# Softmax of a sparse attention: exponential by blocks on ScalarE, with bias and sum

## Chip, cores and metric

One core of one Trainium2 chip. The metric is the device time of one execution in microseconds, the median of the runs. The engines are named as in the profile: PE (matrix product), DVE (vector), ACT (scalar, activations), POOL (GpSimd) and SP (which only issues transfers here).

## What is computed

Attention with two sparse masks over 4 batches, 8 heads, 576 positions and 64 channels, and behind it four experts, each two matrix products, on the 2,304 rows that come out.

```python
def _attn_ref(q, k, v):
    B, H, S, D = q.shape
    stride, scale = 32, 1.0 / np.sqrt(D)
    scores = scale * np.matmul(q, k.transpose(0, 1, 3, 2))
    rel = pos[:, None] - pos[None, :]
    mask_local = (rel >= 0) & (rel < stride)
    mask_strided = (rel >= 0) & (pos[None, :] % stride == pos[:, None] % stride)
    scores = np.where(masks, scores, -1000000000.0)      # heads 0-3 local, 4-7 strided
    scores = scores - np.max(scores, axis=-1, keepdims=True)
    attn = np.exp(scores)
    attn = attn / (np.sum(attn, axis=-1, keepdims=True) + 1e-09)
    return np.matmul(attn, v)

def _moe_ref(x, domain_probs, w1, w2):
    p = domain_probs / (domain_probs.sum(-1, keepdims=True) + 1e-09)
    for e in range(E):
        h = np.maximum(x @ w1[e], 0.0)
        out += p[:, e:e + 1] * (h @ w2[e])
```

## The kernel before

The attention is cut into 16 pairs (n in the code), each two heads of one batch: "L" pairs with the local mask, "S" pairs with the strided one. `plan_pair` plans the work of one pair. Because the masks are sparse, a pair computes only small blocks of scores: an L pair has 9 blocks of 128 rows by 63 keys, an S pair 12 blocks of 128 rows by 54 keys. The softmax of a pair is worked in two groups, of 6 and 3 blocks (L) or 6 and 6 (S), so there are 32 groups in all. The tile pm (pmL or pmS, two buffers of each kind) holds the blocks of a pair, mx their row maxima, sm their row sums.

The steps of a group are, by the names of the functions: `scores` (small matmuls on PE into one or two banks of the pool sc), `mask` (DVE adds the mask, out of PSUM into pm, L541), `rmax` (DVE, the row maxima, L544), `bsub` (DVE or POOL subtracts the maximum of its row, L547), `ex` (ACT, one exponential over the whole group with the factor scale, L551), `rsum` (DVE, the row sums and their reciprocals, L556 to L559; the 1e-9 is an extra column of pm that is set at the start), `norm` (DVE or POOL multiplies by the reciprocal, L562). Then PE transposes three blocks at a time (`tp`, L592), ACT or DVE copies them to pT (`ep`, L452 or L454), PE multiplies with v (`pv`, L622 and L630), and the outcome is copied out as input of the experts.

Of the 2,304 rows the first 384 are worked first, by three-pass products on a high and a low half of each number: xh (the copy on ACT, L671) and xl (the remainder on DVE, L674). The channels of a row come from four pairs, xh_215 to xh_218. The weights are loaded to raw_202 (first layer) and raw_203 (second layer) and split likewise: s_80 and a_77 to a_79 for the first layer, w2t for the second (ACT, then DVE or POOL, L706 and L707). L801 is the first-layer product of these 384 rows, hs its ReLU (L805, L808), and L817 the second-layer product. In the first pass over the weights the channels are taken one after the other in the order of the pairs, so that the products can begin before all four pairs are done. The other rows (896 and 1,024) are worked by a scheme with seven half-size products (L970), once the attention is complete.

A planner in the kernel (`Plan`) sets the order in which the instructions are issued on every engine. Each step is added with its engine, its assumed duration, what it reads and writes and a priority; `walk` replays the engines with these durations and each engine takes what can start first, by priority. Attention steps and MoE steps take turns on PE by a running credit (MIX, SWING). A step of kind VP goes to DVE or POOL, one of kind AD to ACT or DVE, whichever is done sooner by the assumed times. A table SHIFT moves single steps by their number. As long as PE has nothing to do in the start, the planner puts in dummy matmuls on a tile wz, "fillers" (L1282). The order that comes out is fixed when the program is built; every engine then works its own list in that order.

Of the kernel before, what the change touches and what calls it, by code (L numbers as in the profile page):

```python
# [11 lines left out]
AF = mybir.ActivationFunctionType  # L12
# [4 lines left out]

MIX = 0.85
ZN = 30
# [5 lines left out]

LEAD = 8.24
LAG = 1.8
STEADY = 30.04


SHIFT = {
# [6 lines left out]
}  # L38
# [6 lines left out]
class Plan:  # L45
# [8 lines left out]
    DEEP = 1.27  # L54
    ROW = 1.98
    SWITCH = 0.17
    FIRST = 10
    SWING = 4.72
    ENGINES = ("PE", "ACT", "DVE", "POOL", "SP")
# [269 lines left out]
def attn_moe_kernel(  # L329
# [130 lines left out]
    def plan_pair(n):  # L460
# [19 lines left out]

        def pmv(g0, g1, eps=0):
            if kd == "S":
                return pmx[:, g0:g1, 0:W]
            a = pmx[:, P * g0 + 1 - eps:P * g0 + 2 - eps]
            return bass.AP(a.tensor, a.offset, [list(a.ap[0]), [3 * P, (g1 - g0) // 3], [P + 32, 3], [1, W + eps]])

# [11 lines left out]
        for gi, (g0, g1) in enumerate(GRP[kd]):  # L498
# [34 lines left out]
            def mask(key, g0, g1):  # L533
                ng = g1 - g0
                s = held[key][:, 0:ng * W]
                if kd == "S":
                    m, s = m_str.unsqueeze(1).to_broadcast([P, ng, SR]), s.rearrange("p (g w) -> p g w", w=W)
                else:
                    m = m_loc[:, 0 if g0 == 0 else 3:3 if g0 == 0 else 6, :].rearrange("p (v r) w -> p v r w", r=3)
                    s = s.rearrange("p (v r w) -> p v r w", r=3, w=W)  # L540
                nc.vector.tensor_tensor(out=pmv(g0, g1), in0=s, in1=m, op=ALU.add)  # L541

            def rmax(g0=g0, g1=g1):
                nc.vector.tensor_reduce(out=rows(mx, g0, g1), in_=pmv(g0, g1), op=ALU.max, axis=AX.X)  # L544

            def bsub(e, g0=g0, g1=g1, ng=ng):
                engine(e).tensor_tensor(  # L547
                    out=pmv(g0, g1), in0=pmv(g0, g1), in1=per(mx, g0, g1), op=ALU.subtract)

            def ex(g0=g0, g1=g1):  # L550
                nc.scalar.activation(out=pmv(g0, g1), in_=pmv(g0, g1), func=AF.Exp, scale=scale)  # L551

            def rsum(g0=g0, g1=g1):
                r = sm[:, par, g0:g1]
                if kd == "L":
                    nc.vector.tensor_reduce(out=rows(sm, g0, g1), in_=pmv(g0, g1, 1), op=ALU.add, axis=AX.X)  # L556
                else:
                    nc.vector.tensor_reduce(out=r, in_=pmx[:, g0:g1, 0:W + 1], op=ALU.add, axis=AX.X)
                nc.vector.reciprocal(out=r, in_=r)  # L559
# [8 lines left out]
            if kd == "S" and gi == 0:  # L568
                add("PE", 0.9, scores, [f"qkS{bf}{i}" for i in range(2)], keys + [f"pmS{bf}{i}" for i in range(2)], z + 3, keys,
                    cols=4 * nel)  # L570
            elif kd == "L":
                add("PE", (0.5, 0.46)[gi], scores, [f"qkL{bf}{gi}"], keys + [tok], z + 3, keys, cols=4 * nel)
            for i, x in enumerate(keys if kd == "L" else [key]):
                a0, a1 = (g0 + 3 * i, g0 + 3 * i + 3) if kd == "L" else (g0, g1)
                add("DVE", (a1 - a0) * W / 960 + 0.15, lambda x=x, a0=a0, a1=a1: mask(x, a0, a1), [x, "mask" + kd], [tok], z + 3.2)
            add("DVE", dd, rmax, [tok], [tm], z + 3.4)
            add("VP", vp, bsub, [tm], [tok], z + 3.6)
            add("ACT", nel / 1200 + 0.2, ex, (), [tok], z + 3.8)
            add("DVE", dd + 0.25, rsum, [tok], [ts], z + 4)
            add("VP", vp, norm, [ts], [tok], z + 4.2)  # L580

# [21 lines left out]
        for gi in range(2):  # L603
# [56 lines left out]
            if kd == "L":  # L660
                add("PE", 0.15 + 0.165 * ng, pv, need + [f"vstL{bf}{gi}"], keys, z + 7, keys, cols=ng * 288)
            elif gi == 0:
                add("PE", 0.95, pv, need + [f"vstS{bf}{i}" for i in range(2)], keys, z + 7, keys, cols=ng * 182)
            for (t0, nt, nm) in ((0, TA, "x"), (T0[1], TBS[0], "r1"), (T0[2], TBS[1], "r2")):
# [619 lines left out]
    with tc.manual_schedule():  # L1284
        nc.vector.memset(wz, 0.0)
        make_identity(nc, ident)
        for t in pm["S"]:
            nc.gpsimd.memset(t[:, :, SR + 1:64], 0.0)
            nc.gpsimd.memset(t[:, :, SR:SR + 1], 1e-9)
        for t in pm["L"]:  # L1290
            nc.gpsimd.memset(t, 0.0)
            a = t[:, 0:1]
            nc.gpsimd.memset(bass.AP(a.tensor, a.offset, [list(a.ap[0]), [3 * P, 3], [P + 32, 3], [1, 1]]), 1e-9)
        plan.run(idle)
# [76 lines left out]
```

## Time and profile before

| | us |
|---|---|
| median of 3 runs | 795.29 (795.02 to 797.27) |
| profiled execution, its own time | 795.16 |
| its span, first to last instruction | 793.4 |
| PE busy | 784.8 |
| DVE busy | 602.7 |
| POOL busy | 366.1 |
| ACT busy | 330.6 |

The own time of the profiled execution is 1.8 us longer than its span, which runs from the first to the last instruction. Busy times are shares of the span that an engine spends in instructions; idle time of an engine that is not waited for costs nothing. Rows of a trace give starts in microseconds from the start of the span; where neighbours on one engine overlap, the distance from start to start is shorter than a row's duration.

### The profile page before, as it was taken

The page shows a single profiled execution, that of the slowest core. Times are in us where ns is not written, and L with a number is a line of the kernel's source. Part 1 is how long each engine was busy: PE and PEld are TensorE (multiplying, and loading weights), DVE is VectorE, ACT ScalarE, POOL GpSimd, SP SyncE. Part 2 cuts the span into 40 slices and gives each one's busy share as a digit, 9 for nine tenths or more (in the row PEclk, how much of TensorE's full clock was granted, in tenths as well). Part 3 has the DMA queues.
Part 4 walks back from the last instruction along what each step waited for, and adds up shares of the span by engine and source line. Part 5 has one row for each costly group of instructions (what it writes and reads, how often), then busy time and mean ns, then how long its engine had stood idle before and what let it go on. Part 6 is the DMA issues. An engine that isn't in the chain of part 4 may idle for free.

```text
span 793.4 us, 13252 instructions
## 1 busy us (share of the span) xinstructions
PE 784.8 (99%) x5038; PEld 667.8 (84%) x5038; DVE 602.7 (76%) x854; ACT 330.6 (42%) x617; POOL 366.1 (46%) x289
## 2 busy tenths in 40 slices
PE   8999999999999999999999999999999999999998
PEld 5887889889888888898988888888888887888886
DVE  6987877774888686867778593958787868687986
ACT  4656556442635344363535352524141423232330
POOL 6555227650665152534435270708180817171672
PEclk9999999999999999999999999999999999999999
DMA  9586443366769786875863405837384746455525
GB/s 344 197 315 217 163 154 107 109 220 233 271 243 332 248 322 217 311 252 227 296 219 99 182 32 183 293 135 272 134 272 148 243 161 238 176 196 190 181 79 186
DMA packets 70431, 166.59 MB, mean 210 GB/s; under 512 B 5184, under 2 KB 23776, under 8 KB 70368
## 3 DMA queue, kind: packets, MB, share of 16 engines
q1 hardware_dynamic: 70224, 165.63, 59.1%
q8 instruction: 40, 0.66, 0.3%
q14 instruction: 23, 0.19, 0.1%
q10 hardware_dynamic: 144, 0.11, 0.1%
HBM read 105.94 MB, written 59.79 MB: 209 GB/s over the span
## 4 chain that ended last, share of the span: by engine, by line
PE 97%; DMA 1%; DVE 1%; issue 0%; ACT 0%
PE mo L970 22%; PE mo L817 18%; PE ps L970 17%; PE sc L970 15%; PE mo L801 9%; PE ps L817 5%; PE sc L817 5%; PE ps L592 2%; PE ps L630 1%; DMA ring<-d23s 1%; PE sc L529 1%; PE ps L622 1%; PE sc L517 1%; PE mo L1282 1%; DVE wv L707 0%
## 5 line engine op out<-in xcount | busy, mean ns | idle before, releaser
L1035 POOL TENSOR_TENSOR q<-q,q 128x512 f32<-128x512 f32 x41 | 60.9, 1492 | 143.1 <-DVE q L1004 142.2
L817 PE MATMUL mo<-w2t,h 128*128 128x512 f32 x336 | 80.8, 389 | 0.0
L817 PEld LDWEIGHTS mo<-w2t,h 128*128 128x128 f32 x336 | 63.1, 188 | 13.0
L817 PE MATMUL mo<-w2t,hs 128*128 128x512 f32 x288 | 70.0, 396 | 0.0
L808 DVE SCALAR_TENSOR_TENSOR h<-c,h 128x448 fp32r<-128x448 f32 x48 | 60.6, 1289 | 2.3 <-ACT h L805 1.0
L817 PEld LDWEIGHTS mo<-w2t,hs 128*128 128x128 f32 x288 | 52.9, 188 | 11.2 <-DVE hs L808 0.3
L706 ACT ACTIVATE w2t<-raw 128x512 fp32r<-128x512 f32 x60 | 37.2, 630 | 44.1 <-PE mo L817 29.0
L1084 DVE TENSOR_TENSOR acc<-sc,acc 128x512 f32<-128x512 f32 x58 | 39.1, 685 | 17.1 <-PE sc L970 17.0
L1001 DVE TENSOR_TENSOR q<-ps,v 128x512 f32<-128x512 f32 x48 | 33.1, 690 | 25.0 <-PE ps L970 24.8
L707 POOL TENSOR_TENSOR a<-raw,a 128x512 fp32r<-128x512 f32 x17 | 27.0, 1590 | 53.3 <-DVE c L1173 38.4
L826 DVE SCALAR_TENSOR_TENSOR acc<-mo,pr,acc 128x512 f32<-128x512 f32 x45 | 33.6, 747 | 23.2 <-PE mo L817 23.1
L707 POOL TENSOR_TENSOR w2t<-raw,w2t 128x512 fp32r<-128x512 f32 x20 | 28.6, 1436 | 44.9 <-ACT w2t L706 43.9
L992 ACT ACTIVATE v<-mo 128x512 f32<-128x512 f32 x48 | 28.5, 593 | 48.3 <-PE mo L970 48.3
L801 PE MATMUL mo<-xh,a 128*128 128x384 f32 x192 | 45.7, 341 | 0.0
L1004 DVE SCALAR_TENSOR_TENSOR q<-q,pb 128x512 f32<-128x512 f32 x48 | 42.8, 891 | 1.6
L706 ACT ACTIVATE wv<-tmp 128x512 fp32r<-128x512 f32 x32 | 20.1, 631 | 53.7 <-POOL tmp L714 11.0
L817 PE MATMUL ps<-w2t,h 128*128 128x512 f32 x168 | 40.4, 389 | 0.0
L817 PE MATMUL sc<-w2t,h 128*128 128x512 f32 x168 | 40.4, 389 | 0.0
L1030 ACT ACTIVATE Tb11h<-q 128x512 fp32r<-128x512 f32 x16 | 10.0, 628 | 71.2 <-DVE q L1004 71.2
L707 DVE TENSOR_TENSOR w2t<-raw,w2t 128x512 fp32r<-128x512 f32 x40 | 34.1, 881 | 4.9 <-ACT w2t L706 4.8
L1035 DVE TENSOR_TENSOR q<-q,q 128x512 f32<-128x512 f32 x23 | 32.7, 1420 | 6.7 <-POOL Tb21l L1031 6.5
L817 PEld LDWEIGHTS ps<-w2t,h 128*128 128x128 f32 x168 | 31.5, 188 | 6.5
(272 smaller groups left out, 2089.9 us busy)
## 6 DMA issues: line engine op xcount, KB each, us to landing
raw<-in_w SPq DMA_DIRECT2D x28, 1024.0 KB, 5.8
qkS<-in_qk_strided SPq DMA_DIRECT2D x16, 329.0 KB, 5.4
out<-acc SPq DMA_DIRECT2D x18, 256.0 KB, 2.0
qkL<-in_qk_local SPq DMA_DIRECT2D x8, 400.0 KB, 6.6
vstL<-in_v_local SPq DMA_DIRECT2D x8, 384.0 KB, 6.1
vstS<-in_v_strided SPq DMA_DIRECT2D x8, 384.0 KB, 7.4
pb<-dp SPq DMA_DIRECT2D x5, 512.0 KB, 7.4
raw<-in_w SPq DMA_DIRECT2D x4, 512.0 KB, 7.8
```

Of the source, the lines that this page charges most:

```text
L706: add("ACT", 0.62, lambda: nc.scalar.activation(out=hi(), in_=src(), func=AF.Copy), need, [name + "h"], z)
L707: add("VP", VP, lambda e: engine(e).tensor_tensor(out=lo(), in0=src(), in1=hi().bitcast(F32), op=ALU.subtract), need + [name + "h"], [name ...
L801: nc.tensor.matmul(pt[:, 0:TA], w[:, c % 2, (f % 2) * P:(f % 2) * P + P], (xl if i == 1 else xh)[c], start=j == 0, stop=j == 11)
L808: nc.vector.scalar_tensor_tensor(out=dst(), in0=src(), scalar=0.0, in1=hi().bitcast(F32), op0=ALU.max, op1=ALU.subtract)
L817: nc.tensor.matmul(pt, ht[f][:, ts], wt[f][:, cs], start=j == 0, stop=j == 11)
L826: nc.vector.scalar_tensor_tensor(out=a, in0=pt, scalar=sc, in1=a, op0=ALU.mult, op1=ALU.add)
L970: nc.tensor.matmul(pt, a[i == 2][:, j, f * P:f * P + P], skewed(b[i == 1][j], TH), start=bool(first) and n == 0, stop=True, skip_group_che ...
L992: add("ACT", TH2 / 1200 + 0.18, lambda: nc.scalar.activation(out=late["u"][i], in_=held[key][:, 0:TH2], func=AF.Copy), [key, "late3"], [f" ...
L1001: add("DVE", DD, lambda: nc.vector.tensor_tensor(out=q(), in0=src(), in1=late["u"][i], op=ALU.add), [key, f"u{i}", "late3"], [tok], min(zz ...
L1004: add("DVE", DD, lambda: nc.vector.scalar_tensor_tensor(out=q(), in0=q() if from_q else src(), scalar=0.0, in1=late["p"][:, c * TH2:c * TH ...
L1035: add("VP", VP, lambda e: engine(e).tensor_tensor(out=dst[0](), in0=a[0](), in1=b[0](), op=ALU.subtract), [a[1], b[1]], [dst[1]], zz - 2.4)
L1084: add("DVE", DD, lambda i=i, key=key: nc.vector.tensor_tensor(out=acc[i], in0=held[key][:, 0:TH2], in1=acc[i], op=ALU.add), [key], tok, zd)
```

## The change

The mask step multiplies by scale on the way (one instruction with two operations), so pm holds scaled, masked scores; the masked value goes from -8e9 to -1e9. The maximum is written negated. The subtraction `bsub` is gone. `ex` is now a loop over the blocks of the group: one ACTIVATE per block, with the negated maximum as bias per partition and the row sum as a second output. `rsum` no longer sums: it adds 1e-9 and takes the reciprocal. The extra column of 1e-9 in pm is gone. In the planner the assumed durations of these steps follow, some constants and the table SHIFT are other ones, and the order on all engines comes out differently.

```diff
-MIX = 0.85
+MIX = 0.83
...
-    SWING = 4.72
+    SWING = 7.96
...
-                nc.vector.tensor_tensor(out=pmv(g0, g1), in0=s, in1=m, op=ALU.add)
+                nc.vector.scalar_tensor_tensor(out=pmv(g0, g1), in0=s, scalar=scale, in1=m, op0=ALU.mult, op1=ALU.add)
 
             def rmax(g0=g0, g1=g1):
-                nc.vector.tensor_reduce(out=rows(mx, g0, g1), in_=pmv(g0, g1), op=ALU.max, axis=AX.X)
-
-            def bsub(e, g0=g0, g1=g1, ng=ng):
-                engine(e).tensor_tensor(
-                    out=pmv(g0, g1), in0=pmv(g0, g1), in1=per(mx, g0, g1), op=ALU.subtract)
+                nc.vector.tensor_reduce(out=rows(mx, g0, g1), in_=pmv(g0, g1), op=ALU.max, axis=AX.X, negate=True)
 
             def ex(g0=g0, g1=g1):
-                nc.scalar.activation(out=pmv(g0, g1), in_=pmv(g0, g1), func=AF.Exp, scale=scale)
+                for g in range(g0, g1):
+                    o = P * g + 32 * (g % 3) + 1 if kd == "L" else 0
+                    a = pmx[:, o:o + W] if kd == "L" else pmx[:, g, 0:W]
+                    nc.scalar.activation(out=a, in_=a, func=AF.Exp, bias=mx[:, par, g:g + 1], accum_out=sm[:, par, g:g + 1])
 
             def rsum(g0=g0, g1=g1):
                 r = sm[:, par, g0:g1]
-                if kd == "L":
-                    nc.vector.tensor_reduce(out=rows(sm, g0, g1), in_=pmv(g0, g1, 1), op=ALU.add, axis=AX.X)
-                else:
-                    nc.vector.tensor_reduce(out=r, in_=pmx[:, g0:g1, 0:W + 1], op=ALU.add, axis=AX.X)
+                nc.vector.tensor_scalar_add(out=r, in0=r, scalar1=1e-9)
                 nc.vector.reciprocal(out=r, in_=r)
...
             add("DVE", dd, rmax, [tok], [tm], z + 3.4)
-            add("VP", vp, bsub, [tm], [tok], z + 3.6)
-            add("ACT", nel / 1200 + 0.2, ex, (), [tok], z + 3.8)
-            add("DVE", dd + 0.25, rsum, [tok], [ts], z + 4)
+            add("ACT", ng * (W / 1200 + 0.18), ex, [tm], [tok, ts], z + 3.8)
+            add("DVE", 0.3, rsum, (), [ts], z + 4)
             add("VP", vp, norm, [ts], [tok], z + 4.2)
```

The new order is read at two places. On ACT, from the first exponential of the program, before (pmL_242 and pmL_243 are the pm buffers of the first two L pairs, pmS_244 and pmS_245 those of the S pairs):

```order
L551 ACTIVATE pmL_242<-pmL_242 128x2x3x63
L551 ACTIVATE pmL_243<-pmL_243 128x2x3x63
L452 ACTIVATE pTL<-ps 128x384 x2
L551 ACTIVATE pmL_242<-pmL_242 128x3x63
L551 ACTIVATE pmS_244<-pmS_244 128x6x54
L671 ACTIVATE xh_215<-ps 128x384
L452 ACTIVATE pTL<-ps 128x384
L551 ACTIVATE pmS_244<-pmS_244 128x6x54
```

and with the change, from the same place:

```order
L553 ACTIVATE pmL_242,sm<-pmL_242,mx 128x63 x6
L553 ACTIVATE pmL_243,sm<-pmL_243,mx 128x63 x6
L455 ACTIVATE pTL<-ps 128x384
L553 ACTIVATE pmS_244,sm<-pmS_244,mx 128x54 x6
L553 ACTIVATE pmL_242,sm<-pmL_242,mx 128x63 x3
L553 ACTIVATE pmS_244,sm<-pmS_244,mx 128x54 x6
L669 ACTIVATE xh_215<-ps 128x384
L704 ACTIVATE s_80<-raw_202 128x512
L704 ACTIVATE a_77<-raw_202 128x512
```

Each group is now 3 or 6 instructions, and one of the two copies to pTL has gone to DVE. Further on in the same list of the change, up to the copy xh_216:

```order
L553 ACTIVATE pmS_245,sm<-pmS_245,mx 128x54 x6
L553 ACTIVATE pmL_243,sm<-pmL_243,mx 128x63 x3
L455 ACTIVATE pTS<-ps 128x384
L704 ACTIVATE a_78<-raw_202 128x512
L553 ACTIVATE pmS_245,sm<-pmS_245,mx 128x54 x6
...
L704 ACTIVATE w2t<-raw_203 128x512 x2
L455 ACTIVATE pTS<-ps 128x384
L553 ACTIVATE pmL_242,sm<-pmL_242,mx 128x63 x6
L669 ACTIVATE xh_216<-ps 128x384
```

Before, xh_216 stood ahead of the exponentials of pmS_245; now it stands behind nine groups, the last of them of the next L pair. On DVE, from the first mask, with the change:

```order
L544 SCALAR_TENSOR_TENSOR pmL_242<-sc,both 128x3x63 x2
L547 TENSOR_REDUCE mx<-pmL_242 128x6
L544 SCALAR_TENSOR_TENSOR pmL_243<-sc,both 128x3x63 x2
L557 TENSOR_SCALAR sm<-sm 128x6
L558 RECIPROCAL sm<-sm 128x6
L547 TENSOR_REDUCE mx<-pmL_243 128x6
L544 SCALAR_TENSOR_TENSOR pmS_244<-sc,both 128x6x54 x2
```

Before, the maximum of pmL_243 stood ahead of the sum and the reciprocal of pmL_242; now it stands behind the addition and the reciprocal, which wait for ACT. On SP the second load of raw_202 moves behind the loads of v of the second L and the second S pair.

## Rows read from the trace of the kernel before

**Rows 1.** The page's first part: busy us, share of the span, instructions.
```profile
PE 784.8 (99%) x5038; PEld 667.8 (84%) x5038; DVE 602.7 (76%) x854; ACT 330.6 (42%) x617; POOL 366.1 (46%) x289
```

**Rows 2.** Waits of PE: line, released by: us in total, times, longest us.
```profile
PE ps L630 <- issue: 1.2, 2, 0.9
PE mo L1282 <- DVE wz L1285: 1.2, 1, 1.2
PE ps L592 <- DVE xl L674: 0.7, 1, 0.7
PE ps L630 <- ACT pTL L452: 0.5, 2, 0.3
```

**Rows 3.** Three stretches: length, busy us of each engine (instructions), clock, DMA share, GB/s.
```profile
5.80:36.40 30.60, 28.70 (x647) 22.64 (x647) 27.99 (x69) 19.89 (x45) 19.05 (x22) 1.00 0.85 307
36.40:122.00 85.60, 84.67 (x1325) 72.77 (x1324) 67.05 (x154) 48.64 (x106) 33.13 (x42) 1.00 0.55 197
122.00:793.40 671.40, 666.86 (x3060) 570.88 (x3058) 507.37 (x632) 260.62 (x466) 310.64 (x211) 1.00 0.59 207
```

**Rows 4.** Timeline of PE: start us, us, instruction, form, count.
```profile
19.26 0.44 PE L801 MATMUL mo<-xh,a 128*128 128x384 f32 x1
...
26.17 0.44 PE L801 MATMUL mo<-xh,a 128*128 128x384 f32 x1
...
29.12 0.44 PE L801 MATMUL mo<-xh,a 128*128 128x384 f32 x1
...
33.10 0.44 PE L801 MATMUL mo<-xh,a 128*128 128x384 f32 x1
...
36.45 3.92 PE L817 MATMUL mo<-w2t,hs 128*128 128x512 f32 x16
...
72.56 0.71 PE L630 MATMUL ps<-pTL,vstL 128*64 128x96 f32 x11 [0.86 <-issue]
```

**Rows 5.** Timeline of DVE: the softmax of the first group.
```profile
7.25 0.55 DVE L544 TENSOR_REDUCE mx<-pmL 128x6 f32<-128x378 f32 x1
7.83 0.56 DVE L547 TENSOR_TENSOR pmL<-pmL,mx 128x378 f32<-128x378 f32 x1
...
9.41 0.54 DVE L556 TENSOR_REDUCE sm<-pmL 128x6 f32<-128x384 f32 x1
9.98 0.19 DVE L559 RECIPROCAL sm<-sm 128x6 f32<-128x6 f32 x1
```

**Rows 6.** Timeline of ACT in the first 34 us.
```profile
2.46 0.20 ACT L1212 ACTIVATE warm<-wz 128x1 f32<-128x1 bf16 x1
...
12.81 0.36 ACT L551 ACTIVATE pmL<-pmL 128x189 f32<-128x189 f32 x1
13.06 0.48 ACT L551 ACTIVATE pmS<-pmS 128x324 f32<-128x324 f32 x1
...
14.75 0.49 ACT L452 ACTIVATE pTL<-ps 128x384 f32<-128x384 f32 x1
15.14 0.47 ACT L551 ACTIVATE pmS<-pmS 128x324 f32<-128x324 f32 x1
...
18.19 1.14 ACT L706 ACTIVATE a<-raw 128x512 fp32r<-128x512 f32 x2
...
22.92 0.35 ACT L682 ACTIVATE xr<-ps 128x108 f32<-128x108 f32 x1
...
23.47 0.39 ACT L682 ACTIVATE xr<-ps 128x108 f32<-128x108 f32 x1
```

**Rows 7.** Chain that ended last, two pieces: start us, us, line, matmuls.
```profile
130.10 8.34 PE mo L801 x48
138.45 8.20 PE mo L817 x36
```

**Rows 8.** ACT's busy us in the exponentials (L551) alone, in two stretches.
```profile
5.80:36.40 30.60, 4.40 (x10) 1.00 0.85 307
36.40:122.00 85.60, 9.98 (x22) 1.00 0.55 197
```

More of the change, by code (lines that the diff above doesn't have):

```diff
@@ L24 @@
 Z0, ZU = 24.03, 27.0
-LEAD = 8.24
-LAG = 1.8
-STEADY = 30.04
+LEAD = 13.63
+LAG = 1.91
+STEADY = 41.13
 SHIFT = {
[6 rows of a table removed]
[9 rows of a table added]
 }
@@ L54 @@
     DEEP = 1.27
-    ROW = 1.98
+    ROW = 1.95
     SWITCH = 0.17
     FIRST = 10
-    SWING = 4.72
+    SWING = 7.96
     ENGINES = ("PE", "ACT", "DVE", "POOL", "SP")
@@ L479, in plan_pair, with pmv @@
         pmx = pm[kd][bf]
-        def pmv(g0, g1, eps=0):
+        def pmv(g0, g1):
             if kd == "S":
                 return pmx[:, g0:g1, 0:W]
-            a = pmx[:, P * g0 + 1 - eps:P * g0 + 2 - eps]
-            return bass.AP(a.tensor, a.offset, [list(a.ap[0]), [3 * P, (g1 - g0) // 3], [P + 32, 3], [1, W + eps]])
+            a = pmx[:, P * g0 + 1:P * g0 + 2]
+            return bass.AP(a.tensor, a.offset, [list(a.ap[0]), [3 * P, (g1 - g0) // 3], [P + 32, 3], [1, W]])
         def per(a, g0, g1):
@@ L568, in plan_pair @@
             if kd == "S" and gi == 0:
-                add("PE", 0.9, scores, [f"qkS{bf}{i}" for i in range(2)], keys + [f"pmS{bf}{i}" for i in range(2)], z + 3, keys,
+                add("PE", 0.88, scores, [f"qkS{bf}{i}" for i in range(2)], keys + [f"pmS{bf}{i}" for i in range(2)], z + 3, keys,
                     cols=4 * nel)
             elif kd == "L":
-                add("PE", (0.5, 0.46)[gi], scores, [f"qkL{bf}{gi}"], keys + [tok], z + 3, keys, cols=4 * nel)
+                add("PE", (0.68, 0.46)[gi], scores, [f"qkL{bf}{gi}"], keys + [tok], z + 3, keys, cols=4 * nel)
             for i, x in enumerate(keys if kd == "L" else [key]):
@@ L662, in plan_pair @@
             elif gi == 0:
-                add("PE", 0.95, pv, need + [f"vstS{bf}{i}" for i in range(2)], keys, z + 7, keys, cols=ng * 182)
+                add("PE", 0.88, pv, need + [f"vstS{bf}{i}" for i in range(2)], keys, z + 7, keys, cols=ng * 182)
             for (t0, nt, nm) in ((0, TA, "x"), (T0[1], TBS[0], "r1"), (T0[2], TBS[1], "r2")):
@@ L1287, in attn_moe_kernel @@
         for t in pm["S"]:
-            nc.gpsimd.memset(t[:, :, SR + 1:64], 0.0)
-            nc.gpsimd.memset(t[:, :, SR:SR + 1], 1e-9)
+            nc.gpsimd.memset(t[:, :, SR:64], 0.0)
         for t in pm["L"]:
             nc.gpsimd.memset(t, 0.0)
-            a = t[:, 0:1]
-            nc.gpsimd.memset(bass.AP(a.tensor, a.offset, [list(a.ap[0]), [3 * P, 3], [P + 32, 3], [1, 1]]), 1e-9)
         plan.run(idle)
@@ L1351 @@
     add("in_w2", inputs["moe_w2"])
-    NEG = np.float32(-8e9)
+    NEG = np.float32(-1e9)
     zero = np.float32(0.0)
```

15 rows, old and new, of the table SHIFT are left out of this document.

## Prediction

> **What bounds the kernel now.** I read the page's busy times first, then TensorE's waits, then three stretches, then the start engine by engine. The page gives PE 99% of the span [rows 1], and the four longest entries of its waits [rows 2] add up to 3.6 us. The three stretches [rows 3] say where anything can be won. From 122 us to the end PE is busy 666.86 of 671.40 us, and the last 4 us of that are the final addition and the store of the output; the steps that the change edits are over by then. From 36.4 to 122 us the attention pairs are woven into the MoE products and PE is busy 84.67 of 85.60 us. The granted clock is 1.00, its 2.4 GHz level, in all three. The MoE matmuls are 3,360 in both kernels, the attention's are the same too, and of fillers there are 20 for 21. So the time is a fixed amount of PE work plus what PE loses, and it loses only while it has no MoE work: until the first four attention pairs are through softmax. The first MoE matmul is at 19.26 us; the group on xh_217 follows at 26.17, the group on xh_216 at 29.12, that on xh_218 at 33.10, and the first second-layer product at 36.45 [rows 4]. From 29.12 us on PE is hardly ever without work. **The change is worth what it does to those times**, and to the waits of the stretch to 122 us.
>
> **What the change takes away.** Of 32 softmax groups each loses its subtraction (25 on POOL, 7 on DVE) and its sum on DVE. For the first group the subtraction is 0.56 us between maximum and exponential, and the sum is 0.54 us before the reciprocal [rows 5]; both stand on the chain from the scores to the transposes. Everywhere but in the start they are hidden behind MoE matmuls and are worth nothing on PE. POOL gets shorter by 25 subtractions and DVE by 32 sums, which buys nothing by itself, since POOL and DVE are not what the stretch to 122 us waits for; some normalizations, copies to pT and copies to xr move to DVE in exchange. The moved weight load (the second half of raw_202 now goes behind two v loads on SP, 768 KB) lands later, but its first reader, the split a_78, stands far down ACT's queue (below), so I cost it at nothing; without that cover it would be 2.5 us, 768 KB at the 307 GB/s of that stretch [rows 3].
>
> **What it adds.** ACT gets 168 exponentials of 54 or 63 elements instead of 32 of 189 to 378, each with a bias per partition and a sum to write. No row of before shows such an instruction, so its price P, from one start to the next, is bounded. From below: a 189-element exponential is followed by the next instruction after 0.25 us, a 384-element copy after 0.39 us [rows 6], hence 0.7 ns an element and 0.16 us at 63 elements, if bias and sum are free. From above: the ACTIVATE of one element lasts 0.20 us and two of 512 end 1.14 us after the first starts, at 0.52 us from start to start [rows 6]; a whole exponential of 63 is then 0.20 + 0.05 = 0.25 us, and if the sum must be read out by a step of its own, as long as the shortest row, P = 0.45 us. I take **0.33 us**: the exponential's whole 0.25, because its sum cannot be read before its last element, plus the shortest row's 0.20 less the 0.11 by which neighbours overlap (0.36 - 0.25 for the 189-element row).
>
> The Trainium skill (ScalarE: Activation LUTs, What ACT_TABLE_LOAD costs) puts an ACTIVATE with a bias pointer at 280 ns plus 0.833 ns an element and lets neighbours overlap by 93 ns. By that, an estimate, P would be 0.24 us without any reading of the sum, and the sum below would come out 4.3 us lower. No run here shows it yet.
>
> **The start, on ACT's queue.** The order shows what ACT has in front of the copy xh_216, on which the MoE group of 29.12 us rests: nine groups of exponentials, 48 instructions, where before there were fewer and larger ones. I add them up. The first maximum ends at 7.25 + 0.55 = 7.80 us [rows 5], so the first exponential starts at 7.9. The exponentials are 48 x 0.33 = 15.8 us. One wait of 1.0 us lies between the first group and the second: on DVE the second maximum now stands behind the addition of 1e-9 and the reciprocal, which wait for the first group's end (7.9 + 2.0 = 9.9; two small steps of 0.19 [rows 5], then 0.55 for the maximum, gives 10.9). The rest before xh_216 is five 384-element copies at 0.39, seven splits of 512 at 0.52 and two pairs of xr and xh_217 copies at 0.55 (22.92 to 23.47 us [rows 6]): 1.95 + 3.64 + 1.10 = 6.7 us. Start of xh_216: 7.9 + 15.8 + 1.0 + 6.7 = 31.4 us. With 0.49 for the copy [rows 6] and about 0.55 for its remainder on DVE (the nearest DVE row of that size), PE has the group at 32.5 us instead of 29.12. From there to the second-layer product the PE order holds the same pieces less three matmuls: before 36.45 - 29.12 = 7.33 us, of which 0.52 for the three matmuls (8.34 us for 48 [rows 7], 0.17 each). So that product starts at 32.5 + 6.8 = 39.3 us, against 36.45: **+2.8 us**, and ten attention matmuls more of 314 are left to do behind it, 0.1 to 0.2 us. The order's one filler less is worth as much the other way; I count +2.7 us. Each 0.01 us of P is 0.5 us of it; the break-even is P = 0.27. The same check by sums: ACT is busy 19.89 of 30.60 us there [rows 3], 4.40 of it for ten exponentials [rows 8]; 51 at 0.33 us are 16.8, which makes 32.3 of 30.6 us. ACT, which had slack, becomes the engine that the start waits for.
>
> **The stretch to 122 us.** Here 117 small exponentials take the place of 22 that were 9.98 us [rows 8]: 38.6 us, so ACT goes from 48.64 to about 72 us (by the order ten copies to pT and xr, 5 us, go to DVE) of some 88. That is no bound by itself, but ACT works strictly in order, its ReLUs and splits stand behind bursts of 6 to 18 exponentials, and DVE now waits in its own queue for each burst before the reciprocal, with MoE remainders behind it. A late burst costs PE only the first time, since PE's delay gives everything behind it slack. Bounds 0 and 4 us; I take +1.0, about the length of one wait of today [rows 2]. Against it, the longest wait of today behind the start, 0.9 us before a product with v at 72 us [rows 2, 4], belongs to an order of instructions that is gone: -0.9, with 0 as the other end.
>
> **Sum.** 795.16 us is the profiled execution's own time, 0.13 below the median of the three runs. 795.16 + 2.7 + 1.0 - 0.9 = 798.0 us, 0.3% above the median.
>
> **Rivals.**
> *The small exponential is cheap* (P at 0.16 to 0.27). For it: issue intervals of ACT in the trace are far below its durations [rows 6], and subtraction and sum are really off the chain. At P = 0.25, the whole exponential with its sum read out for nothing, the second-layer product starts 48 x 0.08 = 3.8 us earlier than forecast, at 35.5, ahead of today's 36.45; with no new wait in the stretch to 122 us, 798.0 - 3.8 - 1.0 = 793.2, taken as 793. It ends on the other side of the forecast and decides at P = 0.27. Against it: a sum has to leave the engine somewhere. At still lower P there is no more to win than PE's waits and fillers of the start: 0.7, 0.5 and 0.3 us of waits [rows 2] and nine fillers behind the first eleven at 0.23 (8.20 us for 36 of that size [rows 7]), 3.6 us: 791.6 us at best.
> *The late start is absorbed.* PE already pauses in the start (0.7 us for xl, 0.5 for pT, 0.3 before a product with v [rows 2]) and fills with dummy matmuls; if ACT's other pieces run closer together than their rows, the extra is eaten there: about 795.5 us. Against it: ACT's queue has no idle left in my sum.
> *ACT binds the whole attention.* At P = 0.45 the start loses 5.8 us more, and 117 x 0.45 = 52.7 us makes ACT 86 of 88 us to the end of the attention, so that PE waits there again and again: 798.0 + 5.8 = 803.8, some 804 us. For it: ACT was idle 10.7 of 30.60 us in the start [rows 3], waiting for others in its strict order, and would be so again. It decides where ACT's busy share between 36 us and the last pair passes nine tenths.
>
> **How the numbers follow.** A measurement of this kernel can tell about 0.3% (2.4 us) from no change. Forecast, P near 0.33: 0.45, most of it slower (0.37), the rest same (0.08). Cheap: 0.32, faster 0.21 and same 0.11, because 793 lies just above the line at 792.9. Absorbed: 0.12, same. Bound throughout: 0.11, slower. Faster 0.21, same 0.31, slower 0.48. The range runs from the cheap case at its best, 791.6, to 803.0, short of the dear price; some 2 in 10 lie outside: that price, and what is in no case here. The forecast's own range is 795.5 to 801.
>
> **What would show it.** Start to start, the small exponentials 0.33 us apart; a separate read-out row on ACT, or none. First MoE matmul at about 22 us, after 27 exponentials, for 19.26; the xh_216 group at 32.5; the second-layer product at 39.3. ACT nearly without idle between 11 and 32 us. ACT's busy time up by some 25 to 45 us, POOL's down by over 15, and the time after the attention unchanged to a few tenths. The forecast is wrong if the second-layer product starts before 37 us, or if PE's new waits lie behind 40 us rather than before.

## Result and the profile after

The changed kernel takes 802.51 us (median of 4 runs, 802.10 to 804.21), the kernel before 795.58 us beside it. The ratio is 1.0088, 95% interval 1.0066 to 1.0109: slower by 7.0 us, inside the range given, by 0.5 us, and on the likelier of the sides. The size was forecast too small: 798.0 us, 2.7 us above the median of before, and the forecast's own range of 795.5 to 801 does not hold the measured time.

The profiled execution is the longest of the four, 804.21 us with a span of 802.4 us at a mean granted clock of 0.995; the two at 1.000 have spans of 800.3 and 800.5 us. So of the 9.0 us between the two profiled spans about 2 us belong to that execution alone, and the text below takes them out where it can.

The page's first part, against [rows 1]:

```profile
PE 787.6 (98%) x5033; PEld 669.9 (83%) x5037; DVE 600.5 (75%) x876; ACT 363.9 (45%) x906; POOL 336.8 (42%) x246
```

ACT has 33.3 us and 289 instructions more, POOL 29.3 us less, DVE 2.2 us less. 336 instructions on ACT are new: 168 exponentials and 168 steps of another kind, which the timeline of ACT shows (start us, us, instruction, form), against [rows 6]:

```profile
8.03 0.35 ACT L553 ACTIVATE pmL<-pmL,mx 128x63 f32<-128x63 f32 x1 [5.36 <-DVE mx L547]
8.28 0.19 ACT L553 ACTIVATION_READ_ACCUMULATOR pmL<-pmL,mx 128x1 f32 x1
8.37 0.33 ACT L553 ACTIVATE pmL<-pmL,mx 128x63 f32<-128x63 f32 x1
...
9.69 0.33 ACT L553 ACTIVATE pmL<-pmL,mx 128x63 f32<-128x63 f32 x1
...
11.58 0.35 ACT L553 ACTIVATE pmL<-pmL,mx 128x63 f32<-128x63 f32 x1 [1.46 <-POOL pmL L561]
...
28.68 0.57 ACT L669 ACTIVATE xh<-ps 128x216 fp32r<-128x216 f32 x1 [1.10 <-DVE xl L672]
...
34.20 0.49 ACT L669 ACTIVATE xh<-ps 128x384 fp32r<-128x384 f32 x1 [0.26 <-PE ps L628]
```

From 8.03 to 9.69 are five steps: 0.33 us from start to start, and each sum is read out by an instruction of its own. Line 34.20 is the copy xh_216.

TensorE's timeline in the start, against [rows 4]: the first group of MoE matmuls, the group on xh_217, that on xh_216, the second-layer product; between them the longest wait, with the row of the kernel before that answers to it in the second fence.

```profile
22.48 0.42 PE L799 MATMUL mo<-xh,a 128*128 128x384 f32 x1
...
28.79 0.52 PE L590 MATMUL ps<-ident,pmL 128*128 128x128 f32 x3 [1.58 <-DVE xl L672]
...
31.09 0.67 PE L799 MATMUL mo<-xh,a 128*128 128x384 f32 x1
...
36.53 0.44 PE L799 MATMUL mo<-xh,a 128*128 128x384 f32 x1
...
43.19 3.06 PE L815 MATMUL mo<-w2t,hs 128*128 128x512 f32 x12
...
796.74 0.61 PE L968 MATMUL sc<-Tt4h,ring 128*128 128x512 f32 x2
```

```profile
24.38 0.52 PE L592 MATMUL ps<-ident,pmS 128*128 128x128 f32 x3 [0.72 <-DVE xl L674]
...
788.92 0.61 PE L970 MATMUL sc<-Tt4h,ring 128*128 128x512 f32 x2
```

The windows of the changed kernel (length, busy us of PE, its weight loads, DVE, ACT, POOL with instructions, clock, DMA share, GB/s), against [rows 3]; then ACT's exponentials alone in the start, against [rows 8]:

```profile
26.50:30.00 3.50, 1.86 (x77) 1.34 (x77) 3.40 (x10) 2.40 (x8) 1.52 (x2) 0.97 0.25 23
30.00:34.00 4.00, 4.00 (x30) 3.58 (x32) 2.85 (x8) 3.55 (x16) 1.02 (x1) 0.60 0.65 248
...
43.20:137.20 94.00, 92.42 (x1378) 78.11 (x1372) 69.55 (x175) 72.55 (x309) 14.69 (x15) 1.00 0.53 189
```

```profile
5.80:36.40 30.60, 17.39 (x102) 0.89 0.73 267
```

And PE's waits (line, released by: us in total, times, longest), against [rows 2]:

```profile
PE ps L590 <- DVE xl L672: 2.9, 2, 1.6
PE ps L590 <- POOL pmL L561: 2.8, 2, 1.9
```

From these starts, those of [rows 4, 7], the first exponential (8.48 us before) and the chain's block of 48 first-layer matmuls behind the attention (138.86 us now, 130.10 before), the 9.0 us are laid out without a gap:

| us | before | changed | difference |
|---|---|---|---|
| to the first exponential | 8.48 | 8.03 | -0.45 |
| from there to the second-layer product | 27.97 | 35.16 | +7.19 |
| from there to the 48 matmuls | 93.65 | 95.67 | +2.02 |
| from there to the end of the last matmul | 659.43 | 658.49 | -0.94 |
| from there to the end of the span | 3.87 | 5.05 | +1.18 |

The first row differs among executions that have the same work ahead of it (7.31 to 8.23 us among seven kernels of the changed order), so later starts are counted from the first exponential.

**Where the start goes.** The chain that ended last, from the first exponential on (start us, us, what):

```profile
8.03 2.10 ACT pmL L553 x12
...
10.73 0.83 POOL pmL L561
...
11.58 2.09 ACT pmL L553 x12
...
14.05 1.94 ACT pmS L553 x12
15.98 0.99 ACT pmL L553 x6
16.98 1.94 ACT pmS L553 x12
...
20.37 2.05 ACT pmS L553 x12
22.42 0.99 ACT pmL L553 x6
...
24.30 1.10 ACT pmS L553 x7
25.41 0.84 ACT pmS L553 x5
```

42 exponentials (each x2 with its read-out) are 14.04 us of the 18.2 us to 26.25; the kernel before has ACT at 0% of its chain, this one at 5%. Then the chain leaves ACT, and DVE's queue carries it on, against [rows 5]:

```profile
26.27 0.17 DVE L557 TENSOR_SCALAR sm<-sm 128x6 f32<-128x6 f32 x1 [0.90 <-ACT pmS L553]
26.48 0.19 DVE L558 RECIPROCAL sm<-sm 128x6 f32<-128x6 f32 x1
26.58 0.18 DVE L1216 TENSOR_REDUCE psums<-prs 128x18 f32<-128x72 f32 x1
...
27.32 0.88 DVE L1219 TENSOR_TENSOR pr<-prs,psums 128x72 f32<-128x72 f32 x1
28.12 0.52 DVE L672 TENSOR_TENSOR xl<-ps,xh 128x216 fp32r<-128x216 f32 x1
```

DVE stands at the small addition until ACT has ended the last group of pmS_245. Behind it wait the normalization of the experts' probabilities (L1216 to L1219, 26.58 to 28.12: 1.54 us) and xl_217, for which PE waits until 28.79. Both rows name ps: the transposes that wait get a bank of ps from which xl_217 has first to be read. That is 4.41 us later than the last wait of the kernel before, 24.38. From 28.79 PE needs 14.40 us to the second-layer product, where it needed 12.07 from 24.38. For 1.55 us of these 2.33 the clock answers: at 30 to 34 us it is 0.60, mostly its 1.2 GHz level, after PE had been busy for 1.86 of 3.50 us. The first experiment below has the same order on PE at clock 1.00, with 12.85 us from its last wait (24.62) to that product (37.47). The other 0.78 is work that the new order puts ahead: by PE's two lists six transposes and 16 products with v more, 24 matmuls for scores less, and one filler less. So 4.41 + 0.78 + 1.55 = 6.74 us, which is the first two rows of the table.

### The profile page after: what moved, and what is told of

The parts are those of the page before. It is cut to its first block, busy times and chain, and to the rows that moved or that the text cites. A ratio compares the mean times of both kernels' runs of the same rounds, so it can differ in the third digit from the quotient of the medians.

```text
span 802.4 us, 13482 instructions
## 1 busy us (share of the span) xinstructions
PE 787.6 (98%) x5033; PEld 669.9 (83%) x5037; DVE 600.5 (75%) x876; ACT 363.9 (45%) x906; POOL 336.8 (42%) x246
## 4 chain that ended last, share of the span: by engine, by line
PE 92%; ACT 5%; DVE 2%; issue 0%; POOL 0%; ACTq 0%; POOLq 0%; DVEq 0%
PE mo L968 22%; PE ps L968 17%; PE mo L815 16%; PE sc L968 15%; PE mo L799 8%; PE ps L815 5%; PE sc L815 5%; ACT pmS L553 2%; PE ps L590 1%; ACT pmL L553 1%; PE ps L628 1%; PE mo L1280 1%; PE sc L532 1%; PE ps L620 1%; PE sc L520 1%
## 5 line engine op out<-in xcount | busy, mean ns | idle before, releaser
L705 POOL TENSOR_TENSOR a<-raw,a 128x512 fp32r<-128x512 f32 x19 | 29.4, 1548 | 58.5 <-DVE c L1171 47.5
L705 POOL TENSOR_TENSOR w2t<-raw,w2t 128x512 fp32r<-128x512 f32 x14 | 19.6, 1400 | 61.9 <-ACT w2t L704 34.5
```

Source lines behind the costliest of these rows:

```text
L705: add("VP", VP, lambda e: engine(e).tensor_tensor(out=lo(), in0=src(), in1=hi().bitcast(F32), op=ALU.subtract), need + [name + "h"], [name ...
```

## The experiments

Twelve kernels in three sets, each set with the kernel before beside it (795.26, 795.24 and 795.04 us). The theory that stood after the traces: the small exponentials' price on ACT, paid in the start, is the loss. The rivals: the order that came with the change, the table SHIFT, the stretch behind the start. Ratios are to the kernel before; 0.1% is 0.8 us. In the four kernels that leave sums out, POOL also sets sm to 1.0 once at the start, which the edits below do not show.

**One exponential per group, in the changed order.**

```diff
-                for g in range(g0, g1):
-                    o = P * g + 32 * (g % 3) + 1 if kd == "L" else 0
-                    a = pmx[:, o:o + W] if kd == "L" else pmx[:, g, 0:W]
-                    nc.scalar.activation(out=a, in_=a, func=AF.Exp, bias=mx[:, par, g:g + 1], accum_out=sm[:, par, g:g + 1])
+                nc.scalar.activation(out=pmv(g0, g1), in_=pmv(g0, g1), func=AF.Exp, bias=mx[:, par, g0:g0 + 1], accum_out=sm[:, par, g0:g0 + 1])
```

> The changed kernel with its order kept on every engine, but each softmax group takes one exponential again: over the whole group, with the maximum of its first block as bias and one sum for all; it leaves out the other blocks' maxima and sums. Theory A (the price of 168 small exponentials with their read-outs on ACT's queue makes the loss): 32 instructions take the place of 336, ACT is no longer what the start waits for, the second-layer product starts at or before 36.5 us and the time falls to 793 to 796 us. Theory B (the new order of the queues makes the loss, whatever the exponentials cost): the time stays at 799 us or more.

Measured: 796.14 us, ratio 1.0009 (0.9999 to 1.0019). The trace has PE's last wait of the start and the second-layer product at:

```profile
24.62 0.52 PE L587 MATMUL ps<-ident,pmL 128*128 128x128 f32 x3 [0.98 <-DVE xl L669]
...
37.47 8.50 PE L812 MATMUL mo<-w2t,hs 128*128 128x512 f32 x36
```

The product starts 29.42 us after the first exponential; at 37.47 us it is a microsecond later than theory A had it, and the time is 0.1 us above that theory's range. So 6.3 us of the 7.0 (0.79% of 795) go with the number of exponentials. The order by itself costs 0.7 us, no more than its interval, although the end of this kernel is as long as the changed kernel's (5.11 us behind the last matmul, for 3.87 before).

**Sums of the last block only; bias of the first block only.** Both keep 168 exponentials. The first:

```diff
-                    nc.scalar.activation(out=a, in_=a, func=AF.Exp, bias=mx[:, par, g:g + 1], accum_out=sm[:, par, g:g + 1])
+                    kw = {"accum_out": sm[:, par, g:g + 1]} if g == g1 - 1 else {}
+                    nc.scalar.activation(out=a, in_=a, func=AF.Exp, bias=mx[:, par, g:g + 1], **kw)
```

> The changed kernel with its order kept; 168 exponentials with bias, but only the last block of a group writes its sum, so 136 of 168 read-outs are gone (sums of the other blocks are left out). Theory A: the exponential goes from 0.33 to 0.24 us, 40 read-outs fewer ahead of xh_216 at 0.09 us are 3.6 us; 798 to 800 us. Theory B: 801.5 us or more.

The second:

```diff
-                    nc.scalar.activation(out=a, in_=a, func=AF.Exp, bias=mx[:, par, g:g + 1], accum_out=sm[:, par, g:g + 1])
+                    nc.scalar.activation(out=a, in_=a, func=AF.Exp, accum_out=sm[:, par, g:g + 1], **({"bias": mx[:, par, g:g + 1]} if g == g0 else {}))
```

> The changed kernel with its order kept; 168 exponentials with their sums, but only the first block of a group has the maximum as bias (the maxima of the others are left out). It prices the bias operand: if it costs 0.09 us for each instruction from start to start, theory A gives 798 to 800 us as for the read-outs; if the bias is free, 802 to 803 us. Theory B: 801.5 us or more either way.

Measured: 796.81 us, ratio 1.0019 (1.0008 to 1.0030), and 797.44 us, 1.0023 (1.0012 to 1.0033). The timelines of ACT, without sums and then without bias:

```profile
7.33 1.54 ACT L554 ACTIVATE pmL<-pmL,mx 128x63 f32<-128x63 f32 x6 [4.67 <-DVE mx L547]
...
9.85 1.54 ACT L554 ACTIVATE pmL<-pmL,mx 128x63 f32<-128x63 f32 x6 [0.89 <-DVE mx L547]
```

```profile
7.98 0.24 ACT L553 ACTIVATE pmL<-pmL 128x63 f32<-128x63 f32 x1
8.13 0.19 ACT L553 ACTIVATION_READ_ACCUMULATOR pmL<-pmL 128x1 f32 x1
8.22 0.24 ACT L553 ACTIVATE pmL<-pmL 128x63 f32<-128x63 f32 x1
```

Six without sums take 1.54 us, of which the last is 0.34: 0.24 from start to start. Without bias and with the sums it is again 0.24. So of the 0.33 us the read-out is 0.09 and the bias is 0.09, and taking either away wins back 5.2 to 5.5 of the 7.0 us, more than the 2.5 to 4.5 us that the 798 to 800 us expected of both stand for. As 136 of the 168 exponentials lose 0.09, the mean price falls by 0.073: that is 0.7 us for each 0.01 of the price; the prediction had 0.5.

**The probabilities' normalization later on DVE**, behind the remainders, in the changed kernel:

```diff
+    later, done = [], []
...
                             nc.vector.tensor_tensor(
                                 out=cols(xl[c]), in0=src(), in1=cols(xh[c].bitcast(F32)), op=ALU.subtract)
+                            if c == 3 and later:
+                                done.append(c)
+                                if len(done) == 2:
+                                    later.pop()()
...
-    add("DVE", 1.0, normalize, ["prs"], ["pr"], ZN)
+    add("DVE", 1.0, lambda: later.append(normalize), ["prs"], ["pr"], ZN)
```

> The changed kernel with nothing moved but the four DVE instructions that normalize the expert probabilities (L1216 to L1219, 1.55 us): they go from ahead of the first remainder of xh_217 to behind the last one of xh_218. If their place on DVE's queue is a part of the loss (a part of theory B), the group on xh_217 and what follows start 0.8 to 1.5 us earlier: 801.0 to 801.8 us. If ACT alone sets the start (theory A alone): 802.2 to 802.8 us.

Measured: 801.58 us, ratio 1.0078 (1.0063 to 1.0094), 0.8 us under the changed kernel's ratio; the intervals overlap, so this alone proves little. Its trace has PE's last long wait end at 27.39 us, 20.07 after the first exponential (20.76 in the changed kernel), and names what is late next, a split on POOL:

```profile
27.39 0.52 PE L592 MATMUL ps<-ident,pmL 128*128 128x128 f32 x3 [0.90 <-POOL a L711]
```

**The gain side alone: the kernel before without the subtraction, then without the maximum too.** The orders stay as they are; the outputs leave out the subtraction of the maximum.

```diff
             def bsub(e, g0=g0, g1=g1, ng=ng):
-                engine(e).tensor_tensor(
-                    out=pmv(g0, g1), in0=pmv(g0, g1), in1=per(mx, g0, g1), op=ALU.subtract)
+                return
```

> The kernel before with its order kept, and the subtraction of the maximum left out (its 32 instructions on POOL and DVE are not issued, nothing else moves). It prices the gain side of the change alone. If the subtraction stands on the chain that the start waits for, as the 0.56 us of the first group suggests, the second-layer product starts 0.5 to 1 us earlier: 794.3 to 794.8 us. If the start of before waits for weights, DVE and loads instead: 795.0 to 795.6 us. A gain of 2 us or more would say that the change's gain side was underrated.

```diff
             def rmax(g0=g0, g1=g1):
-                nc.vector.tensor_reduce(out=rows(mx, g0, g1), in_=pmv(g0, g1), op=ALU.max, axis=AX.X)
+                return
```

> The kernel before with its order kept; neither the row maximum nor the subtraction is issued, so the exponential takes the scaled and masked scores as they are (left out: the maximum). Theory that the start waits for ACT and PE's own order and not for DVE: 795.0 to 795.6 us, as without the subtraction alone. Rival, DVE's queue in front of the softmax (its maxima, 0.55 us each, ten of them in the start) sets the start: the second-layer product 0.5 to 2 us earlier than in the kernel before, 793 to 794.8 us.

Measured: 795.21 us, ratio 1.0001 (0.9992 to 1.0011), and 795.18 us, 1.0000 (0.9991 to 1.0009). The second-layer product starts at 35.50 us without the subtraction and at 36.02 with both steps gone, instead of 36.45, about what such starts differ by among executions (0.92 us, above), and the time does not move. By these intervals there was at most 0.7 us to win by taking the two steps away. The sum on DVE, which the change takes away as well, was not dropped by itself.

**The same with the order made anew** (the planner is told 0 us for both steps):

```diff
-            add("DVE", dd, rmax, [tok], [tm], z + 3.4)
-            add("VP", vp, bsub, [tm], [tok], z + 3.6)
+            add("DVE", 0.0, rmax, [tok], [tm], z + 3.4)
+            add("VP", (0.0, 0.0), bsub, [tm], [tok], z + 3.6)
```

> As the run before it, with the planner told that maximum and subtraction take no time, so that all queues are ordered anew (left out: the maximum). This is the candidate for a version that beats both kernels. If the order can use the shorter softmax: 792 to 794.5 us. Rival, the table of shifts belongs to the old order and a new order without a new table loses more than it wins (the kernel before without its table takes 799.1): 795.5 to 799 us.

Measured: 796.90 us, ratio 1.0020 (1.0011 to 1.0029). Less work in a new order, and 1.6 us slower, as the rival had it; that the table of shifts belongs to its order is the likely reason, and is not shown by a run of its own. No version that was run beats the kernel before.

**The planner told the price**, in the changed kernel, 0.28 for 0.18 us:

```diff
-            add("ACT", ng * (W / 1200 + 0.18), ex, [tm], [tok, ts], z + 3.8)
+            add("ACT", ng * (W / 1200 + 0.28), ex, [tm], [tok, ts], z + 3.8)
```

> The changed kernel whose planner assumes 0.28 us more than the elements for each small exponential in place of 0.18, so 0.33 us as measured; the order comes out anew, the instructions are the same. If the loss comes from an order made for too cheap an exponential (theory B in its best form), the order now fits and the time falls to 797 to 799 us. If the loss is ACT's work itself (theory A), no order saves it: 801 to 804 us.

Measured: 800.75 us, ratio 1.0074 (1.0061 to 1.0087), 1.1 us under the changed kernel's ratio, with intervals that overlap, and 0.25 us under the range of a loss that no order saves. The trace gives this to the end of the program: 3.82 us from the last matmul to the end of the span, against 5.05 (below). The start is no shorter, 34.70 us from the first exponential to the second-layer product (35.16 in the changed kernel, 33.61 without the 1.55 us of the clock). A better assumed price did not buy anything here.

**Both kernels without the table SHIFT.**

```diff
-SHIFT = {
...
-}
+SHIFT = {}
```

> The kernel before with an empty table SHIFT. The table only moves steps in the order; without it some us are lost, 797 to 803 us. It is the base for the run with the changed kernel's table emptied.

> The changed kernel with an empty table SHIFT. Theory A: the difference to the kernel before without its table is again 5 to 9 us. Theory B (the two tables fit their kernels differently well): the difference is under 3 us.

Measured: 799.08 us, ratio 1.0051 (1.0039 to 1.0063), and 804.55 us, 1.0122 (1.0107 to 1.0138). The change costs 5.5 us between two orders that no table has touched. Their ends are alike (3.83 and 3.89 us behind the last matmul). With tables it is 7.0 us, of which 1.2 lie in the end: 5.8. The loss is not that one table is worse than the other. The planner's other constants stayed as each kernel has them.

**Start and rest apart.** In the changed order one exponential per group, as in the first experiment, for the first five pairs (51 blocks) alone, and then for the other eleven (117 blocks) alone:

```diff
             def ex(g0=g0, g1=g1):
+                if n < 5:
+                    nc.scalar.activation(out=pmv(g0, g1), in_=pmv(g0, g1), func=AF.Exp, bias=mx[:, par, g0:g0 + 1], accum_out=sm[:, par, g0:g0 + 1])
+                    return
```

> The order of the changed kernel; the first five pairs (51 blocks, those of the start) take one exponential per group, the other eleven pairs (117 blocks) keep one per block (left out in the grouped pairs: every block's own maximum and sum but the first's). Theory that the loss arises in the start: 796 to 798 us, near the 796.1 of one exponential per group everywhere. Rival, it arises in the stretch to 137 us, where ACT has 117 small exponentials: 800 us or more.

> The counterpart of the run before it: one exponential per block in the first five pairs only, one per group from the sixth pair on (left out in the grouped pairs: every block's own maximum and sum but the first's). Theory that the loss arises in the start: 800.5 to 802 us. Rival, it arises behind the start: 796 to 798 us. The gains of this run and of the run before it, against the changed kernel, should add up to the 6.4 us of one exponential per group everywhere.

Measured: 798.52 us, ratio 1.0035 (1.0023 to 1.0047), and, with `n >= 5`, 800.62 us, 1.0065 (1.0053 to 1.0077). Grouping the start wins back 0.53%, 4.2 us; grouping the rest 0.23%, 1.8 us; together 6.0 of the 6.3. The theory that the whole loss arises in the start does not hold as it stood: 798.52 us lies 0.5 us above its range. Two thirds are in the start, one third behind it. The stretch behind the start in the two kernels, first with 117 small exponentials in it, then with grouped ones:

```profile
43.20:137.20 94.00, 92.45 (x1380) 78.89 (x1379) 69.01 (x169) 73.41 (x298) 17.05 (x17) 1.00 0.51 180
```

```profile
43.20:137.20 94.00, 94.00 (x1387) 80.51 (x1386) 69.83 (x175) 50.72 (x123) 15.14 (x16) 1.00 0.54 189
```

With 117 small exponentials PE loses 1.55 us there, with one per group none. In the changed kernel these are four waits:

```profile
64.73 0.52 PE L590 MATMUL ps<-ident,pmS 128*128 128x128 f32 x3 [0.24 <-ACT hs L803]
75.42 0.52 PE L590 MATMUL ps<-ident,pmS 128*128 128x128 f32 x3 [0.18 <-ACT pmL L553]
86.34 0.88 PE L628 MATMUL ps<-pTL,vstL 128*64 128x96 f32 x16 [0.45 <-DVE xr L682]
114.62 0.55 PE L590 MATMUL ps<-ident,pmL 128*128 128x128 f32 x3 [0.71 <-ACT xr L680]
```

One, of 0.18 us, names the exponential itself. The other three, 1.40 of the 1.58 us, name ACT's ReLU, ACT's copy to xr and DVE's copy to xr. By their names these have nothing to do with softmax, and all four are gone when the bursts ahead of them are short.

## Why the prediction was right, and where it was too small

**The price** was right: 0.33 us taken, 0.333 us measured at 63 elements and 0.32 at 54, with the separate read-out row of 0.19 us that the upper bound had supposed. The Trainium skill (ScalarE: Activation LUTs, What ACT_TABLE_LOAD costs) gives 93 ns for a pointer operand, and 0.24 us without the read-out was the estimate from its figures. The two experiments without sums and without bias show 0.24 and a bias of 0.09, so the rule agrees, and the read-out is what it leaves open.

**The cheap rival** fell by its price, but its sum would have been wrong too. At 0.24 us it should have given 793 us; the two kernels in which 136 of the 168 have that price take 796.8 and 797.4. Their mean price is 0.26 us, under the break-even of 0.27, and both are slower than the kernel before, by 0.19 and 0.23%, clear of their intervals: the break-even was too high. One exponential per group is less for ACT than the rival at its cheapest (32 at 0.71 us at most, read-out and all, for 168 at 0.16), and takes 796.1: even there nothing is won.

**What the change takes away** was costed at nothing on PE. For the subtraction, and the maximum with it, the runs show the same: ratios 1.0001 and 1.0000; for the sum on DVE it is not shown by itself. The moved weight load, costed at nothing too, held nobody up: no wait of the changed kernel to 44 us names a load of raw. Nor was anything absorbed, as the rival of a hidden start had it: PE's waits grew from 0.7 us [rows 2] to 2.9 us for xl and 2.8 us for POOL's normalizations. POOL fell by 29.3 us and DVE stood in its place: the view of line L553 says who waited for the small exponentials (us, times).

```profile
  DVE sm L557: 17.9, 20
```

DVE waited 17.9 us in 20 pieces for a step that takes 0.17; before, it waited 1.4 us for the exponentials.

**The start** is the step that failed. It was counted at +2.7 us and is +6.74 in the profiled execution, 5.2 without the 1.55 us at the lower clock. By its own marks: the first MoE matmul at 22 us was right (22.48); the copy xh_216 was to start at 31.4 and starts at 34.20; its group was to start at 32.5 and starts at 36.53; the 6.8 us from there to the second-layer product were right (6.66). So the sum behind xh_216 held, and the sum ahead of it did not. It added up ACT's queue alone, with one wait of 1.0 us. Ahead of xh_216 ACT waits four times, 1.46 + 1.10 + 0.39 + 0.26 = 3.2 us, and for the others' queues each time. Above all, xh_216 was not what PE waited for last. That was xl_217, on DVE, behind an earlier piece of ACT's queue: the forecast's own numbers (7.9 + 42 x 0.33 + 1.0 + 2.7 for three copies and three splits) bring ACT to 25.5 us, and from there the changed order leads over DVE's addition, reciprocal, 1.54 us of probabilities and xl_217 to some 28, 28.64 in the trace. From then on PE has no wait, so it is PE's own list, 12.85 us at full clock, that sets the product.

One of the waits was not in the sum at all. The second group's exponential was to wait for its maximum, which ended at 10.97 us:

```profile
10.46 0.51 DVE L547 TENSOR_REDUCE mx<-pmL 128x6 f32<-128x378 f32 x1
```

It started at 11.58, 0.03 us behind the end of POOL's normalization of the first group (10.73 + 0.82). The two groups belong to the L pairs n = 0 and n = 2, and the kernel keeps sm by `par = n % 2`: the normalization still reads sm[:, 0, 0:6], and the exponential now writes its sums into the same columns, so it has to wait. The diff says so, where `ex` has `ts`, the sums, among what it writes. In the kernel without most sums the second group starts at 9.85 (above), behind its maximum, while POOL normalizes from 9.55 to 10.37; there only the sixth exponential of the group, some 1.2 us later, writes a sum. So the second output brought a wait with it, 0.6 us in the start. Columns of their own for the two pairs were not tried.

**The stretch behind the start** was counted at +1.0 - 0.9 and is +2.0 to the end of the attention; the two parts are 2.1 us for the small exponentials (the ratios of the first experiment and of the one with 117 of them) and -0.3 in the first experiment (93.39 us for 93.65), where the old wait is gone and gave back less than its 0.9. The bounds of 0 to 4 held it. ACT's busy share, 72.55 of 94.00 us, is far from the nine tenths of the dear rival, and PE waits all the same, 1.58 us: here an engine that works in order delays others at three quarters busy.

**The end** was taken as unchanged. The last matmuls come 0.94 us sooner after the attention than before, and the store 1.18 us later. That was in no case of the prediction. The store is told in the last section; why the matmuls come sooner stays open.

**The range** held the time by 0.5 us, and that is luck in part: its upper end, 803.0, was set just short of what a price of 0.45 us would give, and neither that price nor ACT at nine tenths came about. What filled the range instead were the waits in the other queues and the end.

## What to carry to other kernels

Six exponentials of 63 with bias and sum take 2.0 us here where one of 378 took 0.52; moving work onto an engine by many small instructions pays only where the steps it relieves are waited for, and dropping those steps outright in a trial (here worth 0.0 us, 0.7 at most) says so before anything else is built. A start is to be followed through every queue that the chain crosses, up to the last wait of the engine that bounds the kernel: adding up the busiest queue alone gave half of it (2.7 of 5.2 us at full clock). When an instruction gets a second output, look at who still reads the columns that it writes.

## What the runs showed of the hardware that was not expected

**An instruction fetch beside the last store.** The DMA view of the last microseconds, from the last matmul on, of the changed kernel and then of the kernel before:

```profile
GB/s 0 0 289 337 418 369 402 225 16 0 0 0 209 273 402 337 386 337 113 0 16 16 0 16 16 16 32 16 0 0 0 0 0 0 0 0 0 0 0 0
...
q8 instruction: 1, 0.02, 1.2%
...
out<-acc SPq DMA_DIRECT2D x1, 256.0 KB, 3.2
```

```profile
out<-acc SPq DMA_DIRECT2D x1, 256.0 KB, 2.0
```

The last store lands 3.2 us after its issue for 2.0: most of it is through as always by 799.8 us, and its last packets come one at a time until 800.9, at 16 or 32 GB/s. They come behind a packet of the queue q8, which loads instructions; it starts between 798.8 and 799.4 us and takes about 1 us (1.2% of 16 engines' 5.1 us). Of the fourteen kernels here, the seven with the changed kernel's order have such a packet in their last 6 us and take 5.05 to 5.24 us behind the last matmul; the other seven have none there and take 3.82 to 3.91.

In the kernel before the last such packet starts between 784.4 and 785.4 us, 8 us ahead of the end. The DMA view of that microsecond shows that the store issued beside it is late as well:

```profile
q8 instruction: 1, 0.02, 9.3%
...
out<-acc SPq DMA_DIRECT2D x1, 256.0 KB, 3.3
```

There nobody waits for the store, and those issued from 787.4 us on land after 2.0 us again. So the late store goes with the packet, and not with the changed order alone. The packet was not moved by an edit of its own, so that it is the cause stays inferred from these rows. The Trainium skill (Runtime: NRT & Kernel Launch, Instruction fetch mechanics) says that an engine's instructions come in blocks of 16 KiB over a DMA queue of its own, and that the cost is mostly hidden. The profile page's 40 packets of q8 with 0.66 MB agree with the size, and the end of this program is a place where the cost is not hidden.

**The price of a sum and a bias on ACT.** The read-out has a row of 0.19 us and costs 0.09 from start to start; a bias per partition lengthens the ACTIVATE from 0.24 to 0.33 us, and costs as much.

**The lower clock in the middle of the start.** The changed kernel leaves PE idle for 1.64 of the 3.50 us to 30 us, and in its profiled execution the clock is 0.60 in the next 4 us, when PE has work without a break: 1.55 us. The same execution is at 0.50 at 12.8 to 16.0 us, ahead of waits for other engines. In two of the four executions the mean clock was 1.000. In the profiled execution of the kernel with one exponential per block in the first five pairs alone, PE has the same gap (2.36 of 4.00 us busy from 26 to 30 us in both), and the clock stays at 1.00 from 30 to 34 us. So a later start can cost more than its own length, in some executions, and the gap alone does not say in which.
